# Weights loaded behind the transposes, row and column groups between the layers, and a rebuilt tail: one change to a tuned two-layer attention and expert kernel

## The chip, the cores and the metric

The kernel runs on one core of a Trainium2 chip. The metric is the device time of one execution in microseconds (us); several executions are timed, and the median and the range are given. A trace of one execution (the profile) comes with each kernel. Its span is the time from the first to the last instruction, 1.7 to 1.8 us less than the time of the same execution.

Engines are named as in the profile: PE is TensorE's matmul, PEld its weight load, DVE is VectorE, ACT is ScalarE, POOL is GpSimd, SP is SyncE, which issues most transfers. "L431" is line 431 of the kernel's source. Lines differ between the kernels, so the text names the operation too. In the cuts of code, `ps(...)` reserves a tile of PSUM, into which products are written.

## The reference, cut to what matters

```python
x = A_x                                                         # 2048 rows of 512, bf16
x = x + _A_ref(_layernorm(x, axis=-1), A_wqkv, A_wo)            # linear attention, 32 heads of 16
x = x + _B_ref(_layernorm(x, axis=-1), B_w_r, B_w_gate, B_w_up, B_w_down)
x = x + _A_ref(_layernorm(x, axis=-1), A_wqkv, A_wo)            # the same weights again
x = x + _B_ref(_layernorm(x, axis=-1), B_w_r, B_w_gate, B_w_up, B_w_down)

# in _A_ref: phi(t) = where(t > 0, t + 1, exp(t)) + 1e-6
kv  = einsum("bhsd,bhse->bhde", phi(k), v)                      # K^T V, a sum over all rows
num = einsum("bhqd,bhde->bhqe", phi(q), kv); den = phi(q) . sum(phi(k)); out = (num / den) @ wo
# in _B_ref: the two rows with the largest x @ w_r go through silu(x w_gate) * (x w_up) @ w_down,
# are scaled by a sigmoid and added back to their own rows
```

Each attention layer needs a sum over all rows (K^T V) before any row of its output can be made, and each expert block needs the top two of all 2,048 rows before it can start. So there are four places where everything waits for something small. The last of them, the second expert block, is the tail of the kernel.

## The kernel before

The kernel records every operation with an estimated duration and a weight, and a list scheduler written in Python puts them in one order. That order fixes the order on each engine. The tokens are sixteen tiles of 128 rows. K, Q and O are the products for keys, queries and outputs, four matmuls of 512 columns a tile (0.86 us). K^T V is formed from G, the products of phi(K) with the normalised rows, and from wv after wv has been centred.

The loads. The last number is the earliest planned time, in us; a transpose writes xnT, the operand of K and Q:

```python
for dst, src, key, kb, after in ((wq, A_wq, "wq", 512, 12.0), (wr, B_wrc, "wr", 1, 9.0), (wot, A_wot, "wot", 512, 24.0),
                                 (wv, A_wv, "wv", 512, 26.0), (wo, A_wo, "wo", 512, 28.0)):
    dma(dst[:], src, [key], kb, after)
...
def trans(t, **k):
    def f():
        nc.sync.dma_start_transpose(out=xnT[:, :, t * P : (t + 1) * P], in_=xn[:, t, 0:D])
    op("SP", 1.3, f, r=[("xn", t)], w=[("xnT", t)], lat=1.35, **k)
```

The K^T V product, sixteen products of 128 columns, once a layer:

```python
for c in range(NC):                     # NC = 4
    for k in range(NC):
        T_.matmul(pv[:, c, :].rearrange("p (b f) -> p b f", b=NC), lhsT=wv[:, k, c * P : (c + 1) * P],
            rhs=GT[:, k, :].rearrange("p (b f) -> p b f", b=NC)[:, :, 32 * c : 32 * (c + 1)],
            start=(k == 0), stop=(k == NC - 1))
```

The correction of layer 2's G for the two rows that the first expert block changed: four rows, so products of which TensorE uses 4 of its 128 rows (`4*128` in the timeline below, 0.97 us from the first of them to what follows the last):

```python
pe(4 * MM, lambda: [
    T_.matmul(G2[c]()[:], lhsT=xr4[:, gcol(c) : gcol(c) + P], rhs=pk4[:], start=False, stop=True) for c in range(NC)
], r=["xr4", "pk4"], w=G2)
```

The tail. The output tiles are stored four at a time (512 KB), and the two expert rows, yo, are stored on top of them at the very end, so that store waits for the four large ones:

```python
gu2 = ps("g", [P, 2, NF, 2])
gate_up(gu2, 6, 2)                       # 88 products of 2 columns, gate and up in one PSUM tile
...
for g in (1, 2, 3):
    for i, t in enumerate(ORD[4 * g : 4 * g + 4]):
        last_out(OUTK[g][i], t, prio=1)
    store(ORD[4 * g], ORD[4 * g] + 4)
...
for q in range(NF):                      # down: 44 products in four column groups
    for g in range(NC):
        T_.matmul(yp()[32 * g : 32 * g + 32, :], lhsT=h2[:, q, :], rhs=wd[:, q, g * P : (g + 1) * P],
            start=False, stop=(q == NF - 1), tile_position=(0, 32 * g))
```

## Time and profile before

| | before |
|---|---|
| time, median of 3 runs (range) | 164.12 us (163.51 to 164.63) |
| traced execution | 162.2 us, span 160.5, mean granted TensorE clock 0.969 |
| first K^T V product, layer 1 | 44.79 us |
| first K^T V product, layer 2 | 119.63 us |
| second top-2 (its last step on TensorE starts) | 148.86 us |
| last 512 KB output store issued | 152.20 us |
| expert rows yo being copied out / row store issued | 156.68 / 157.32 us |
| span | 160.49 us |

The page of the kernel before: each digit is the busy share of a fortieth of the span in tenths, PEclk is the granted TensorE clock in tenths, and the last two lines are the chain of work that ended last, by engine and by line.

```profile
PE   6999999589999999999989999999999999996770
DVE  1599999937899999999989988954398999999940
PEclk9999999999999999999999999999999999999755
## 4 chain that ended last, share of the span: by engine, by line
PE 68%; DVE 19%; DMA 5%; ACT 3%; issue 2%; DVEq 0%
```

TensorE is full almost everywhere. It has one hole near slice 7 (28 to 32 us) and a tail from slice 36, where the clock falls as well. The hole is the one wait of TensorE on a transfer. The waits of TensorE from 24 to 46 us:

```profile
PE mm L431 <- DMA xnT<-xn: 2.3, 1, 2.3
```

K of tile 12 (L431) waits 2.3 us for its transpose. The queue of SP shows why: the two 512 KB loads stand between the ninth and the tenth of these transposes. The columns are start, duration, queue and line, operation and count.

```profile
13.03 13.20 SPq L392 DMA_TRANSPOSE xnT<-xn  x9
26.28 0.57 SPq L221 DMA_DIRECT2D wot<-in_A_wot_dram  x1
26.90 0.42 SPq L221 DMA_DIRECT2D wv<-in_A_wv_dram  x1
27.43 8.12 SPq L392 DMA_TRANSPOSE xnT<-xn  x6
35.59 0.57 SPq L221 DMA_DIRECT2D wo<-in_A_wo_dram  x1
```

The timeline of TensorE, five places of it: K of tile 12, the product that centres wv (L757), the first K^T V (L513), the correction of G (L1249) and the second K^T V.

```profile
32.84 1.04 PE L431 MATMUL mm<-wk,xnT 128*128 128x512 bf16 x4 [2.33 <-DMA xnT<-xn]
...
35.44 0.38 PE L757 MATMUL tp<-wv,elast 128*128 128x512 bf16 x1
...
44.79 1.06 PE L513 MATMUL g<-GT,wv 128*128 128x128 bf16 x16
...
116.72 1.03 PE L1249 MATMUL g<-pk,xr 4*128 4x512 bf16 x4
...
119.63 1.05 PE L513 MATMUL g<-GT,wv 128*128 128x128 bf16 x16
```

And the tail: gate and up (L1018), the first part of down (L1416), then down itself after 1.07 us without work, at half clock (granted 0.50 from 150.38 us to the end).

```profile
151.43 2.53 PE L1018 MATMUL g<-xs,wgu 128*128 128x2 bf16 x88
153.90 0.30 PE L1416 MATMUL g<-ident,xf 128*32 128x128 bf16 x4
155.26 1.36 PE L1422 MATMUL g<-wd,h 128*32 128x128 bf16 x44 [1.07 <-DVE h L1411]
```

### The profile page before, as it was taken

What the parts mean: (1) busy time and instruction counts of PE and PEld (TensorE: products, weight loads), DVE (VectorE), ACT (ScalarE), POOL (GpSimd) and SP (SyncE); (2) the same over time, 40 slices, a digit from 0 to 9 for tenths busy, and PEclk for the clock granted to TensorE, in tenths of its full rate; (3) what the DMA queues carried; (4) which work ended last, traced back from release to release, by engine and by line L of the source; (5) the groups of instructions that cost most, each with busy time, mean ns of one, the idle gap of its engine ahead of it and who ended that gap; (6) DMA issues with size and microseconds to landing.
All of it is one profiled execution on the core that took longest, in us unless ns stands there. A gap on an engine that the chain in (4) does not pass through costs nothing.

```text
span 160.5 us, 3799 instructions
## 1 busy us (share of the span) xinstructions
PE 148.6 (93%) x1332; PEld 75.5 (47%) x1332; DVE 132.7 (83%) x481; ACT 108.9 (68%) x263; POOL 23.5 (15%) x66
## 2 busy tenths in 40 slices
PE   6999999589999999999989999999999999996770
PEld 2344444144454444444435445576455455555660
DVE  1599999937899999999989988954398999999940
ACT  3269999625568678889979555543268997798900
POOL 7413113000000000040140300200100000363000
PEclk9999999999999999999999999999999999999755
DMA  4999784978991000033144540000000000012550
GB/s 116 353 355 319 202 97 94 278 152 300 421 432 63 0 0 4 2 64 66 29 73 100 100 99 2 6 0 4 0 0 4 0 4 0 2 50 87 202 192 2
DMA packets 24499, 17.15 MB, mean 107 GB/s; under 512 B 17952, under 2 KB 22560, under 8 KB 24096
## 3 DMA queue, kind: packets, MB, share of 16 engines
q1 hardware_dynamic: 24184, 16.39, 36.1%
q10 hardware_dynamic: 296, 0.53, 1.0%
q8 instruction: 10, 0.16, 0.4%
q14 instruction: 9, 0.07, 0.2%
HBM read 10.62 MB, written 2.10 MB: 79 GB/s over the span
## 4 chain that ended last, share of the span: by engine, by line
PE 68%; DVE 19%; DMA 5%; ACT 3%; issue 2%; DVEq 0%
PE mm L477 15%; PE g L463 13%; PE g L606 9%; PE mm L431 7%; DVE x L615 6%; PE mm L444 5%; DMA xnT<-xn 5%; PE tp L807 3%; DVE pk L409 2%; DVE pq L592 1%; PE g L1018 1%; PE tp L569 1%; PE tp L1018 1%; PE g L551 1%; DVE em L402 1%
## 5 line engine op out<-in xcount | busy, mean ns | idle before, releaser
L398 ACT ACTIVATE e<-mm 128x512 bf16<-128x512 f32 x52 | 30.9, 596 | 18.7 <-PE mm L431 9.9
L463 PE MATMUL g<-pk,xn 128*128 128x512 bf16 x128 | 31.9, 379 | 0.0
L477 PE MATMUL mm<-xnT,wq 128*128 128x512 bf16 x128 | 31.6, 379 | 0.0
L606 PE MATMUL g<-KW,pq 128*128 128x512 bf16 (+1 forms) x132 | 30.2, 372 | 0.0
L431 PE MATMUL mm<-wk,xnT 128*128 128x512 bf16 x80 | 19.9, 379 | 3.0 <-DMA xnT<-xn 2.6
L623 ACT ACTIVATE sq<-x 128x512 bf16<-128x512 bf16 (+1 forms) x33 | 20.1, 612 | 3.1 <-DVE x L615 2.7
L402 DVE TENSOR_SCALAR em<-e 128x512 bf16<-128x512 bf16 x52 | 15.3, 303 | 6.7 <-ACT e L398 6.3
L463 PEld LDWEIGHTS <-xn 128*128 128x128 bf16 x128 | 12.0, 98 | 14.3 <-issue 0.4
L606 PEld LDWEIGHTS <-pq 128*128 128x128 bf16 x132 | 12.4, 97 | 13.2
L477 PEld LDWEIGHTS <-wq 128*128 128x128 bf16 x128 | 11.7, 98 | 12.9 <-issue 0.4
L409 DVE SCALAR_TENSOR_TENSOR pk<-mm,em 128x512 bf16<-128x512 f32 x20 | 13.7, 686 | 0.3
L384 POOL TENSOR_SCALAR xn<-x,s,nb 128x512 bf16<-128x512 bf16 x7 | 5.8, 833 | 56.0 <-DVE nb L371 44.6
L348 DVE BATCH_NORM_STATS2 st<-x 128x6 f32<-128x512 bf16 x16 | 10.3, 677 | 3.3 <-DMA x<-in_A_x_dram 3.3
L431 PEld LDWEIGHTS <-xnT 128*128 128x128 bf16 x80 | 7.3, 97 | 11.9 <-DMA xnT<-xn 4.3
L615 DVE SCALAR_TENSOR_TENSOR x<-x,opr,g 128x512 bf16<-128x512 bf16 (+1 forms) x17 | 11.8, 710 | 0.1
L409 DVE SCALAR_TENSOR_TENSOR pq<-mm,em 128x512 bf16<-128x512 f32 x16 | 10.9, 686 | 0.2
L615 DVE SCALAR_TENSOR_TENSOR x<-x,g 128x512 bf16<-128x512 bf16 x16 | 10.6, 676 | 0.0
L592 DVE TENSOR_TENSOR pq<-pq,rd 128x1024 bf16<-128x1024 bf16 x16 | 10.3, 684 | 0.0
L444 PE MATMUL mm<-wkc,xt 128*128 128x512 bf16 x40 | 9.9, 379 | 0.2 <-DVE pq L409 0.2
L401 ACT ACTIVATE rl<-mm 128x512 bf16<-128x512 f32 x16 | 9.6, 602 | 0.0
L417 ACT ACTIVATE e<-mm,rho 128x512 bf16<-128x512 f32 x12 | 8.3, 689 | 1.6 <-PE mm L450 0.8
L363 ACT ACTIVATE lnv<-mv,eps_t 128x2 f32<-128x2 f32 (+2 forms) x18 | 5.1, 291 | 4.7 <-DVE mv L349 3.9
(249 smaller groups left out, 224.8 us busy)
## 6 DMA issues: line engine op xcount, KB each, us to landing
wgu<-in_B_wgu_dram SPq DMA_DIRECT2D x2, 1408.0 KB, 9.5
out_dram<-pk SPq DMA_DIRECT2D x4, 512.0 KB, 3.2
wd<-in_B_wd_dram SPq DMA_DIRECT2D x1, 1408.0 KB, 13.9
x<-in_A_x_dram SPq DMA_DIRECT2D x4, 256.0 KB, 5.6
xt<-in_A_xt_dram SPq DMA_DIRECT2D x4, 256.0 KB, 5.6
x<-in_A_x_dram SPq DMA_DIRECT2D x2, 512.0 KB, 7.1
wk<-in_A_wk_dram ACTq DMA_DIRECT2D x2, 256.0 KB, 4.1
xt<-in_A_xt_dram SPq DMA_DIRECT2D x1, 512.0 KB, 7.8
```

Of the source, the lines that this page charges most:

```text
L348: dve(0.61, lambda: V.bn_stats(out=st()[:], in_=x[:, t, :]), r=[("x", t)], w=[st]).early = 6.0
L398: act(0.5, lambda: A.activation(out=e()[:], in_=p()[:], func=ACT.Exp), r=[p], w=[e], **k)
L402: dve(0.2, lambda: V.tensor_scalar(out=em()[:], in0=e()[:], scalar1=1.0, scalar2=TINY, op0=ALU.min, op1=ALU.add), r=[e], w=[em], port=True ...
L409: dve(0.6, lambda: V.scalar_tensor_tensor(out=out_ap, in0=p()[:], scalar=0.0, in1=em()[:], op0=ALU.max, op1=ALU.add), r=[p, em], w=[key], **k)
L431: T_.matmul(p()[:], lhsT=xnT[:, c, t * P : (t + 1) * P], rhs=wk[:, c, :], start=(c == 0), stop=(c == NC - 1))
L444: T_.matmul(p()[:], lhsT=xt[:, c, t * P : (t + 1) * P], rhs=w[:, c, :], start=(c == 0), stop=(t >= NM and c == NC - 1),)
L463: T_.matmul(Gs[c]()[:], lhsT=xn[:, t, gcol(c) : gcol(c) + P], rhs=pk[:, t, :], start=first, stop=last)
L477: T_.matmul(p()[:], lhsT=wq[:, i, c, :], rhs=xnT[:, i, j * D : (j + 1) * D], start=(i == 0), stop=(i == NC - 1))
L592: dve(0.6, lambda q=q: V.tensor_tensor(out=q, in0=q, in1=rd()[:].to_broadcast([P, 2, D]), op=ALU.mult), r=[rd], w=[("pq", j, c), ("pq", j, ...
L606: T_.matmul(p()[:, a : a + n], lhsT=pqt(c, t * P, P), rhs=KWs[layer][:, c, a : a + n], start=(c == 0), stop=(c == NC - 1),)
L615: dve(0.04 + 0.6 * n / D, lambda a=a, n=n: V.scalar_tensor_tensor(out=x[:, t, a : a + n], in0=x[:, t, a : a + n], scalar=1.0 if i == 1 els ...
L623: act(0.1 + 0.5 * n / D, lambda a=a, n=n, sq=sq: A.activation(out=sq()[:, 0:n], in_=x[:, t, a : a + n], func=ACT.Square, scale=float(D) ** ...
```

## The change

Its intent: keep large loads out of the way of the transposes; run small products side by side in groups of TensorE's rows or columns; take the patch of x from VectorE; keep TensorE's clock up in the tail; and let SiLU of the gate start while the up products still run. With it came several hundred weights of single operations for the scheduler, found by search, so almost every engine's order differs. Cut to its core:

```diff
-    for ... ((wq, A_wq, "wq", 512, 12.0), ..., (wot, A_wot, "wot", 512, 24.0), (wv, A_wv, "wv", 512, 26.0), (wo, A_wo, "wo", 512, 28.0)):
+    for ... ((wq, A_wq, "wq", 512, 8.0), ..., (wot, A_wot, "wot", 512, 30.0), (wv, A_wv, "wv", 512, 30.0 + 0.5), (wo, A_wo, "wo", 512, 30.0 + 3.0)):
         dma(dst[:], src, [key], kb, after)
     # trans(): the plan now counts a transpose as queued behind loads:  ... lat=1.7).queue = True
@@ K^T V: 32 products of 64 columns, two at a time in two column groups @@
-        p = ps("g")
+        p = ps("g", [P, NC * NC, 1, 16])
         ...
@@ the correction of G: each of its four products in its own group of 32 rows @@
-    pe(4 * MM, lambda: [
-        T_.matmul(G2[c]()[:], lhsT=xr4[:, gcol(c) : gcol(c) + P], rhs=pk4[:], start=False, stop=True) for c in range(NC)
-    ], r=["xr4", "pk4"], w=G2)
+        for c in range(NC):
+            rows = slice(32 * c, 32 * c + 32)
+            T_.matmul(G2[c]()[:], lhsT=xr4[rows, gcol(c) : gcol(c) + P], rhs=pk4[rows, :], start=False, stop=True,
+                tile_position=(32 * c, 0))
@@ the patch of x: VectorE -> ScalarE (out of PSUM) and GpSimd @@
-            V.tensor_tensor(out=xv, in0=xv, in1=pp()[:], op=ALU.add)
+            G_.tensor_tensor(out=xv, in0=xv, in1=ppb[:, j : j + 1, :], op=ALU.add)
@@ the last tile of layer 2 in three pieces, its variance put together in ScalarE's Ln @@
-        parts = ((0, H), (H, H)) if split else ((0, D),)
+        cuts = [0, 256, 384, 512] if split else [0, D]
@@ twelve products on zeros, for the clock alone; gate and up in separate banks, 32 columns wide @@
+    sp_ = ps("mm")
+    for _ in range(12):
+        pe(MM, lambda: T_.matmul(sp_()[:], lhsT=warm[:, 0:P], rhs=warm[:], start=True, stop=True), r=["Odone"], w=[sp_])
-    gu2 = ps("g", [P, 2, NF, 2])
-    gate_up(gu2, 6, 2)
+    gu2 = [ps("g", [P, NF, 32]) for _ in range(2)]
+    gate_up([(p, lambda q, p=p: p()[:, q, :]) for p in gu2], lambda c: xs2[:, c, :], "xs2", 11)
```

## The prediction

> **What bounds the kernel now.** The chain of waits is 68% TensorE, 19% VectorE. Start-to-start gaps of the matmuls show that, from 7 to 145 us, TensorE streams all but about 8.5 us. The windows give three kinds of stage. (a) 24-37 us: TensorE busy 10.5 of 13.0 us. K of tile 12 waits 2.3 us for its DMA transpose, which took 5.4 us to land against a median of 2.5: the 512 KB loads of wot and wv were issued just ahead of it (26.3, 26.9 us). (b) 45-82 and 126-142 us: TensorE and VectorE both full (VectorE 19.9 of 20 us in 62-82). (c) 144.7-160.5 us: a 15.8 us tail of dependent small steps, the granted clock falling to 0.5 at about 150 us.
>
> **What the change does, costed from the trace.**
> 1. wot, wv, wo go behind all sixteen transposes; wq and some x/xt loads change places. In the new SP order the last fourteen transposes are consecutive. At 1.31 us an issue (trace) I estimate tile 12 landing near 31 us instead of 32.8, tile 15 near 35; the first K^T V product then starts near 43 us instead of 44.8. **-1.8 us**, all critical.
> 2. K^T V product in two column groups: 16 x 56 ns = 0.89 us becomes an estimated 0.6, twice. **-0.6 us**.
> 3. The four-row correction of G becomes four row groups: now 4 x 216 ns plus a switch, 0.97 us; concurrent, about 0.35. **-0.6 us**. [...] the trace agrees for column groups: starts 3-4 ns apart, about 60 ns for four.
> 4. x patch from VectorE to ScalarE and GpSimd: 1.4 us of VectorE where it is idle: **0**.
> 5. New order by many weights: stages 45-119 hold about 3.5 us of TensorE gaps; I give it **-0.6 us**.
> 6. Tail. Twelve idle matmuls and 32-column gate/up products should keep the clock at 1.0: down product 1.36 to about 0.9 us, gate/up 2.45 to 2.2. Separate banks let SiLU overlap the up products: 1.3 us between gate/up and down becomes about 0.5. Three pieces and the shorter variance path gain little: VectorE is last there, and added small steps and an output tile stand in its queue. But the final row-store waits for the last 512 KB output store, landed at 157.2 us, as late as the row itself: this caps the gain. **-1.3 us**.
>
> Sum: -4.9 us, so 159.2 us.
>
> **Chances.** 80% range 156.0-162.0. Faster by over 2% (below 160.8): 0.74; within 2%: 0.24; slower: 0.02.
>
> **What would show each step.** (1) K waiting on transposes under 1.2 us, K^T V starting at 42-43.5 us, transposes landing in about 2.5 us. (2) 32 products of 64x64 in about 0.6 us. (3) Row-group products starting a few ns apart, 0.35 us in all. (4) GpSimd's patch done before the first layer-2 denominators. (5) VectorE still 98% busy after the first layer's products. (6) Clock 1.0 to the end; under 0.7 us from last up product to first down product; final row-store issued when the last output store lands.
>
> **What would make it wrong.** wv landing too late, so that the centring product, ahead of two G products in TensorE's queue, stalls it. xt or x of late tiles, issued 4-6 us later, stalling K. The GpSimd patch delaying layer 2. The clock falling all the same. A better order in 45-142 us than I credit: two to three us faster. VectorE's queue delaying the last variance: up to 0.6 us slower.

The 0.35 us of step 3 is an estimate from the trace of before: a 512-column product takes 216 ns, four products of 512 columns in column groups start 3 to 4 ns apart with the next one 217 or 206 ns after the fourth (L551, 122.8 to 123.3 us), and the two intervals around the four-row products are about 90 ns longer than usual (311 ns before the first, 306 after the last). That row groups behave like column groups was not shown there, nor that idle matmuls or 32-column products hold the clock.

## The result

| | before | after | after, second run (c_after) |
|---|---|---|---|
| median (range) | 164.07 us (163.51 to 164.63, 4 runs) | 158.67 us (157.58 to 159.27, 4 runs) | 158.21 us (157.80 to 158.66, 4 runs) |
| traced span, clock | 160.49, 0.969 | 156.90, 0.992 | 155.97, 0.995 |
| first K^T V, layer 1 | 44.79 | 43.16 | 42.42 |
| first K^T V, layer 2 | 119.63 | 116.32 | 115.50 |
| second top-2 | 148.86 | 146.17 | 145.33 |
| last 512 KB store issued | 152.20 | 148.92 | 148.08 |
| yo / row store issued | 156.68 / 157.32 | 153.23 / 153.71 | 151.73 / 152.79 |

The ratio of after to before is 0.966, 95% interval 0.960 to 0.973. A ratio is the mean time of one kernel's fast runs over that of the other's in the same rounds, so it is not quite the ratio of the medians quoted. On the chip of the second run, before took 163.17 us (161.19 to 165.52) and the ratio was 0.975 (0.965 to 0.986). Medians and ranges here and below are of all executions; the ratios leave out those that the record calls slow (three of the seven of before on that chip).

The page of the changed kernel, the lines that were shown of before:

```profile
PE   6989999997999999999999999999999999998970
DVE  1799999776699999999999979853488999999840
PEclk9999999999999999999999999999999999999996
## 4 chain that ended last, share of the span: by engine, by line
PE 72%; DVE 12%; DMA 5%; ACT 5%; issue 3%; SPq 0%; ACTq 0%; DVEq 0%
```

The hole at slice 7 is gone and a shallower one stands at slice 9; the clock holds to the last slice (granted 1.00 until 154.24 us, where it was 150.38). TensorE's waits from 24 to 46 us, and SP's queue:

```profile
PE tp L792 <- DMA wv<-in_A_wv_dram: 1.1, 1, 1.1
```

```profile
13.76 20.48 SPq L402 DMA_TRANSPOSE xnT<-xn  x14
34.29 0.57 SPq L230 DMA_DIRECT2D wv<-in_A_wv_dram  x1
34.92 0.41 SPq L230 DMA_DIRECT2D wot<-in_A_wot_dram  x1
35.38 0.43 SPq L230 DMA_DIRECT2D wo<-in_A_wo_dram  x1
```

The fourteen transposes now go through without a load among them. K of tile 12 starts 3.0 us earlier and waits for nothing, but wv is issued at 34.29 us, and the centring product, moved back in TensorE's order, waits for it. The five places of TensorE's timeline again:

```profile
29.84 1.03 PE L441 MATMUL mm<-wk,xnT 128*128 128x512 bf16 x4
...
38.90 0.38 PE L792 MATMUL tp<-wv,elast 128*128 128x512 bf16 x1 [1.13 <-DMA wv<-in_A_wv_dram]
...
43.16 0.75 PE L525 MATMUL g<-GT,wv 128*64 128x64 bf16 x32
...
113.96 0.40 PE L1294 MATMUL g<-pk,xr 32*128 32x512 bf16 x4
...
116.33 0.69 PE L525 MATMUL g<-GT,wv 128*64 128x64 bf16 x32
```

The correction of G takes 0.40 us instead of 1.03, and K^T V 0.75 and 0.69 instead of 1.06 and 1.05. The tail:

```profile
148.62 2.35 PE L1059 MATMUL g<-xs,wgu 128*128 128x32 bf16 x88 [0.25 <-DVE xs L1417]
150.91 0.24 PE L1476 MATMUL g<-ident,xf 128*32 128x128 bf16 x4
151.64 0.69 PE L1482 MATMUL g<-wd,h 128*32 128x128 bf16 x36 [0.49 <-DVE h L1470]
152.89 0.29 PE L1482 MATMUL g<-wd,h 128*32 128x128 bf16 x8 [0.57 <-issue]
```

Between gate/up and down 0.49 us are idle where it was 1.07, and down runs at full clock (1.00; its groups of four start 56 ns apart, in before 107), but it stops after its 36th product for a reason that the profile can only call "issue". SiLU starts at 150.35 us, 0.45 us before the last up product starts; in before it starts 0.63 us after that (154.43, 153.80). Now, where did the 4 us come from? Subtracting the milestones of the tables:

| stretch | before | after | c_after |
|---|---|---|---|
| start to first K^T V, layer 1 | 44.79 | 43.16 (-1.63) | 42.42 (-2.37) |
| to first K^T V, layer 2 | 74.84 | 73.16 (-1.68) | 73.08 (-1.76) |
| to second top-2 | 29.23 | 29.85 (+0.62) | 29.83 (+0.60) |
| to yo | 7.82 | 7.06 (-0.76) | 6.40 (-1.42) |
| to row store | 0.64 | 0.48 (-0.16) | 1.06 (+0.42) |
| to the end | 3.17 | 3.19 | 3.18 |
| sum | 160.49 | 156.90 (-3.6) | 155.97 (-4.5) |

Two things stand out. Layer 2 up to the second top-2 became slower. And in the second trace, where down did not stop, yo was ready 0.7 us sooner against the top-2, but the row store gained nearly nothing from it: it was waiting for something else.

The two medians differ by more (5.4 us) than the spans. The fast executions of before that were not traced had lower mean clocks than the traced one: 0.955 to 0.965 in the last set of eleven, against 0.969. One more stretch of 3.41 us at half clock, as e_loads_first has one below, lowers the mean over 162 us by 0.5 x 3.41 / 162 = 0.01, so I estimate that before loses up to one such stretch more in many of its runs. No trace of before itself shows one; e_loads_first and b_loads_late show one and two behind a stop of TensorE.

### The profile page after: what moved, and what is told of

Same layout as the page of the kernel before. It is cut to its first block, busy times and chain, and to the rows that moved or that the text cites. A ratio compares the mean times of both kernels' runs of the same rounds, so it can differ in the third digit from the quotient of the medians.

```text
span 156.9 us, 3902 instructions
## 1 busy us (share of the span) xinstructions
PE 147.9 (94%) x1380; PEld 74.4 (47%) x1380; DVE 130.2 (83%) x481; ACT 111.9 (71%) x272; POOL 28.5 (18%) x78
## 4 chain that ended last, share of the span: by engine, by line
PE 72%; DVE 12%; DMA 5%; ACT 5%; issue 3%; SPq 0%; ACTq 0%; DVEq 0%
PE mm L487 18%; PE g L473 17%; PE g L618 11%; PE mm L441 10%; DVE x L628 4%; PE mm L454 4%; DMA wv<-in_A_wv_dram 3%; ACT pk L1334 3%; DMA x<-in_A_x_dram 3%; DVE st L358 2%; DVE pq L604 2%; PE tp L581 1%; PE tp L1059 1%; PE g L563 1%; PE mm L597 1%
## 5 line engine op out<-in xcount | busy, mean ns | idle before, releaser
L408 ACT ACTIVATE e<-mm 128x512 bf16<-128x512 f32 x52 | 30.4, 597 | 12.7 <-PE mm L441 6.7
L618 PE MATMUL g<-KW,pq 128*128 128x512 bf16 (+2 forms) x136 | 30.6, 366 | 0.4 <-DVE x L628 0.4
L636 ACT ACTIVATE sq<-x 128x512 bf16<-128x512 bf16 (+2 forms) x34 | 20.4, 601 | 2.9 <-DVE x L628 2.5
L394 POOL TENSOR_SCALAR xn<-x,s,nb 128x512 bf16<-128x512 bf16 x6 | 4.9, 825 | 52.9 <-PE g L618 37.9
L628 DVE SCALAR_TENSOR_TENSOR x<-x,opr,g 128x512 bf16<-128x512 bf16 (+2 forms) x18 | 11.9, 684 | 0.4 <-PE g L618 0.3
L373 ACT ACTIVATE lnv<-mv,eps_t 128x2 f32<-128x2 f32 (+3 forms) x18 | 5.2, 291 | 5.0 <-DVE mv L359 3.3
```

The source lines that it names most:

```text
L408: act(0.5, lambda: A.activation(out=e()[:], in_=p()[:], func=ACT.Exp), r=[p], w=[e], **k)
L618: T_.matmul(p()[:, a : a + n], lhsT=pqt(c, t * P, P), rhs=KWs[layer][:, c, a : a + n], start=(c == 0), stop=(c == NC - 1),)
L628: dve(0.04 + 0.6 * n / D, lambda q=q, a=a, n=n: V.scalar_tensor_tensor(out=x[:, t, a : a + n], in0=x[:, t, a : a + n], scalar=1.0 if i == ...
L636: act(0.1 + 0.5 * n / D, lambda q=q, a=a, n=n, sq=sq: A.activation(out=sq()[:, 0:n], in_=x[:, t, a : a + n], func=ACT.Square, scale=float( ...
```

## The experiments

All kernels were correct. Each was timed against before on its own chip, so ratios compare best; differences from the changed kernel are read from the traces.

### e_loads_first: the load order undone

wot and wv go back in front of the eleventh transpose. All else stays as in the changed kernel, the late centring product too.

```diff
+        trs = [o for o in seq if o.eng == "SP" and o.w and o.w[0][0] == "xnT"]
+        for key in ("wot", "wv"):
+            o = next(o for o in seq if o.w == (key,))
+            seq.remove(o)
+            seq.insert(seq.index(trs[10]), o)
```

> The changed kernel with one thing undone: the loads of wot and wv stand again ahead of the last six transposes in the SP queue (wo stays behind). Every other engine's order is the same. Theory (step 1 is worth 1.8 us because late loads free the transposes): K of a late tile waits 1.5 to 3 us for its transpose again, the centring product no longer waits for wv, so the first K^T V product starts at 44.0 to 45.0 us instead of 43.2, and the time rises by 1.0 to 1.8 us. Rival (the new order of the other engines, not the load order, made the gain): the first K^T V product starts at 42.5 us or before and the time falls, because wv is no longer waited for.

Measured: 162.61 us (161.33 to 164.40), ratio to before 1.004 (0.992 to 1.016). The gain of the whole change is gone. K of tile 12 waits 2.9 us (2.3 in before), and then something more happens: the first K^T V starts at 46.81 us, 3.65 us later than in the changed kernel and 2 us later than in before. The waits of TensorE from 24 to 50 us, and the windows:

```profile
PE mm L442 <- DMA xnT<-xn: 2.9, 1, 2.9
```

```profile
core 0: us, PE busy (x) PEld busy (x) DVE busy (x) ACT busy (x) POOL busy (x), PEclk, DMA share, GB/s
...
34.00:38.00 4.00, 4.00 (x12) 1.47 (x11) 0.98 (x2) 1.15 (x2) 0.00 (x0) 0.57 0.70 183
```

After the stop of TensorE (3.0 us from one product's start to the next beyond the usual gap) the granted clock is 0.5 from 34.1 to 37.5 us, 3.41 us in which a 512-column product takes 426 ns instead of 215. So this stop cost itself and then half of that stretch, 1.7 us, again. The 2.3 us stop of before cost nothing of the kind: the clock record of its trace stands at 1.00 from 7.02 to 150.38 us. These are single cases; no run shows how long a stop may be. The load order was worth about 4 us here, more than twice what I had predicted.

### e_wv_early: wv from another queue

In the changed kernel wv is loaded from ScalarE's queue at about 20 us, so that it goes ahead of the late transposes without standing in SP's order. In the trace of after the DMA engines are busy for 0.45 of the time from 18 to 24 us.

```diff
+        o = next(o for o in seq if o.w == ("wv",))
+        seq.remove(o)
+        o.fn = lambda: nc.scalar.dma_start(out=wv[:], in_=A_wv)
+        seq.insert(next(i for i, q in enumerate(seq) if q.eng == "ACT" and q.start > 20.0), o)
```

> The changed kernel with the load of wv alone issued at about 20 us from ScalarE's queue, in the stretch where the transposes leave the DMA engines half idle. Theory (the load of wv, queued behind the last transposes, is what the centring product and so all of TensorE waits for, 1.6 us): that wait goes, the first K^T V product starts at 41.5 to 42.2 us instead of 43.2, and the time falls by 1.0 to 1.6 us. Rival (the transposes cannot bear 512 KB among them): a K waits for its transpose by 1 us or more and the K^T V start stays at 43 us.

Measured: 157.98 us (157.89 to 158.09), ratio 0.978 (0.972 to 0.983). TensorE waits for no transfer between 24 and 46 us, and the first K^T V starts at 42.23 us: 0.9 us before the trace of the changed kernel, but only 0.2 us before its second trace, in which the wait for wv was 0.2 us instead of 1.1. So the wait is real but varies, and taking it out is worth 0.2 to 0.9 us, less than the 1.0 to 1.6 expected. K of tile 12 starts at 30.16 us, as in c_after (30.02), so the early load got in no transpose's way.

### e_rows_off: the correction of G in one row group

```diff
-                G2[c]()[:], lhsT=xr4[rows, gcol(c) : gcol(c) + P], rhs=pk4[rows, :], start=False, stop=True,
-                tile_position=(32 * c, 0),
+                G2[c]()[:], lhsT=xr4[0:4, gcol(c) : gcol(c) + P], rhs=pk4[0:4, :], start=False, stop=True,
```

> The changed kernel with the four-row correction of G as four products one after the other on rows 0 to 3, no row groups; all orders the same. Theory: the four products take 0.97 us again instead of 0.33, and everything after them starts 0.6 us later, so +0.6 us in the span of the stretch from the correction to the second K^T V product. Rival (they were not on the critical chain, or the switch cost eats the gain): under 0.3 us.

Measured: 159.54 us (158.15 to 159.97), ratio 0.986 (0.976 to 0.996). From the correction to the second K^T V it is 3.00 us instead of 2.36: the row groups are worth 0.64 us, as predicted. In all ten traces that have both kinds of groups this stretch is 2.36 or 2.37 us. The switch that the prediction and the expectation name stands on both sides with and without row groups: the last start before the four comes 310 ns ahead of them in after and 311 in before, where 215 is usual, and the next start 319 ns after the last of the four in after, 306 in before, instead of 216. In after the four start 3 to 4 ns apart. The whole times of this run and the next are not clear enough of noise to show as little.

### e_cols_off: K^T V without column groups

The sixteen products of 128 columns and their mask are put back.

```diff
-        p = ps("g", [P, NC * NC, 1, 16])
+        p = ps("g")     # and the sixteen products of before
```

> The changed kernel with K^T V as before: sixteen 128-column products instead of thirty-two 64-column ones in two column groups, twice; all orders the same. Theory: each K^T V takes 0.84 us from first to last start instead of 0.55 and 0.50, +0.3 us each; but the grouped form pays a switch of about 0.1 us on each side, so the net is +0.1 to +0.25 us each, +0.2 to +0.5 us in all. Rival (prediction's 0.3 each without switches): +0.6 us in all.

Measured: 159.72 us (158.89 to 160.08), ratio 0.988 (0.980 to 0.995). From the first K^T V product to the first O product it is 7.85 us instead of 7.50 in layer 1 and 7.93 instead of 7.68 in layer 2, 0.6 us in all, as predicted. The switch on each side, in the trace of after: the first product of K^T V starts 308 and 309 ns after the 512-column product before it instead of 215, and the product behind it 130 and 129 ns after its last start, where its pairs start about 32 ns apart. This trace has a stop of 0.9 us at 80 us besides, in front of a K product, which I don't put down to the edit.

### c_after: the changed kernel again

No edit; it stands beside the next three on one chip.

> Control: the changed kernel itself, unaltered, on the chip and in the rounds of the tail experiments. Expected: 157.5 to 159.3 us; in its trace again a stop of 0.4 to 0.8 us after the 36th of the 44 down products, at the same place of TensorE's program (theory: TensorE's instructions run out there[...]). Rival: the stop was a chance event of one execution and is not seen again.

Measured: 158.21 us (157.80 to 158.66), ratio 0.975 (0.965 to 0.986). The stop after the 36th down product, 0.79 us in the first trace, isn't there, against the expectation: down takes 0.66 us from its first to its last start, and yo starts to be copied out at 151.73. But the row store goes out at 152.79, so the end of the kernel moved only by what had been gained before the tail (0.84 us at the last output store).

### e_no_spin and e_no_spin_narrow: the tail without the twelve products on zeros

```diff
-        pe(MM, lambda: T_.matmul(sp_()[:], lhsT=warm[:, 0:P], rhs=warm[:], start=True, stop=True), r=["Odone"], w=[sp_])
+        pe(MM, lambda: None, r=["Odone"], w=[sp_])
@@ e_no_spin_narrow, besides @@
-    gate_up([(p, lambda q, p=p: p()[:, q, :]) for p in gu2], lambda c: xs2[:, c, :], "xs2", 11)
+    gate_up([(p, lambda q, p=p: p()[:, q, 0:2]) for p in gu2], lambda c: xs2[:, c, 0:2], "xs2", 11)
```

> The changed kernel without the twelve idle matmuls of the tail; all other orders the same. Theory: with nothing dense after the last O product the clock falls to 0.5 at 148 to 149.5 us instead of 150 to 153.6; gate/up takes 2.4 us or more instead of 2.2 and the groups of four down products 100 ns instead of 60: 0.4 to 0.8 us longer from the second top-k to the last down product, apart from the stop inside the down products, which should go because TensorE's program is 24 rows shorter (that gives back 0.4 to 0.8, so the total time may hardly move). Rival: the 32-column gate/up products alone hold the clock, and gate/up stays at 2.2 us.

> The changed kernel without the twelve idle matmuls and with gate/up products of 2 columns as before. Theory: the clock is as in the kernel before, mean 0.96 to 0.975, gate/up 2.4 us or more, down groups about 105 ns; 0.5 to 0.9 us slower than without the idle matmuls removed, less the stop. If this equals the run without idle matmuls alone, the 32 columns do nothing for the clock by themselves; if that one keeps the clock and this one does not, they do.

Measured: 158.71 us (158.64 to 158.91) and 158.29 us (157.97 to 159.34), ratios 0.978 and 0.974. Without the twelve products the clock falls to half at 144.3 us (145.3 in the narrow one; I had expected 148 to 149.5) and stays there to the end. The clock line of e_no_spin's page:

```profile
PEclk9999999999999999999999999999999999998555
```

The second top-2 to yo takes 7.50 us instead of 6.40. So they hold the clock here (1.00 in c_after from 140 to 153 us), and that is worth 1.1 us of the chain. The whole time shows no more than half of it: the second top-2 came 0.2 us sooner (29.65 instead of 29.83 us after the second K^T V), and yo has some 0.7 us of slack before the row store in c_after. In both runs the row store goes out 0.13 us after the last 512 KB store has landed, so what the clock is worth once the store is on time was not measured. The 32 columns instead of 2 did nothing measurable here; with the twelve products they were not tried alone.

### e_up_first: the up products ahead of the gate products

All up products of layer 2 are issued ahead of all gate products, so that the separate banks let nothing start early.

```diff
+            if layer2[0]:
+                part = todo[NF:] + todo[:NF] if lo == 0 else []
```

> The changed kernel with the 44 up products ahead of the 44 gate products, so that SiLU can start only after all 88, as when both lay in one bank; all other orders the same. Theory: the time from the last of the 88 products to the first down product grows from 0.83 us to 1.6 to 1.9 us, and the row is stored 0.8 to 1.1 us later; the total time rises by 0.5 to 1.1 us (part may hide behind the last output store). Rival (the ScalarE queue, whose table load and tanh end at 150.4 us, sets when SiLU starts, so the bank split gains little): under 0.4 us.

Measured: 158.10 us (157.75 to 158.30), ratio 0.974 (0.963 to 0.984), the same as c_after. And yet the edit did what it should: from the last gate/up product to the first down product it is 1.78 us instead of 0.84. A delay of 0.94 us in the last chain of the kernel cost nothing that the time shows. So in c_after the chain of small steps did not set the end. What did is the wait for the last 512 KB store: the row store follows its issue by 4.72 us in c_after, and by 4.85 here, where yo starts to be copied out 0.33 us before the row store. In both it goes out 0.13 us after that store has landed; here yo is finished only 0.05 us before it, so the delay has just used up the slack. The queue of SP, from 145 us on, waits for the store before the row store can go (first c_after, then e_up_first):

```profile
SPq L1498 <- DMA out_dram<-pk: 2.8, 1, 2.8
```

```profile
SPq L1500 <- DMA out_dram<-pk: 2.9, 1, 2.9
```

### What holds the last store

That led me to look at the transfers, which I had treated as a fixed latency. The moved data of the changed kernel, in forty slices from the issue of the last output store to that of the row store:

```profile
GB/s 324 341 375 290 384 265 256 290 410 384 299 401 410 384 282 358 341 299 367 282 375 282 256 26 9 26 26 26 17 26 26 26 26 26 17 9 0 0 0 0
...
q8 instruction: 1, 0.02, 1.1%
```

A slice is 0.12 us. For 2.8 us the transfers run at some 340 GB/s, 0.95 MB in all: what is left of the output stores before, and the last one behind it. Then 1.4 us follow at about 22 GB/s, a sixteenth of it, which I read as one of the 16 DMA engines still at work while the others have finished. Each store ends with sixteen 4-byte packets. In the ten traces (before, after twice, and the seven experiments above) fifteen of them are done 2.6 to 2.9 us after the issue and the sixteenth at 4.2 to 4.6 us. The row store goes out about 0.55 us after the sixteenth. And in each of the ten traces one packet of 16 KB on an "instruction" queue lies within that store, and takes 0.88 to 1.57 us:

| | 16 KB packet took | 15 engines done | 16th engine done |
|---|---|---|---|
| before | 1.57 | 2.62 | 4.57 |
| after | 0.88 | 2.83 | 4.25 |
| c_after | 0.88 | 2.85 | 4.20 |
| e_no_spin | 1.24 | 2.84 | 4.47 |

(us after the issue of the last output store, except for the packet's duration.) The engine is late by the packet's time and some 0.4 to 0.5 us more. There are ten such packets in a trace (queue 8: `q8 instruction: 10, 0.16` on the page; the other instruction queue, 14, carried packets of up to 8 KB), and TensorE has by far the most instructions, 2,760 on the page of the changed kernel (1,380 products, each with its weight load; the next is VectorE with 481), so I took them for TensorE's. That could be tested.

### x_warm_30: forty TensorE instructions more at the very start

The ten warm-up products of 512 columns become thirty of 170, the same number of columns less 20. The programs of all other engines and the rest of TensorE's are the same, instruction for instruction.

```diff
-            for _ in range(n):
-                T_.matmul(p()[:], lhsT=warm[:, 0:P], rhs=warm[:], start=True, stop=True)
+            for _ in range(3 * n):
+                T_.matmul(p()[:, 0:170], lhsT=warm[:, 0:P], rhs=warm[:, 0:170], start=True, stop=True)
```

> The changed kernel with the ten warm-up products of 512 columns at the very start cut into thirty of 170 columns: the same work, and 40 more TensorE instructions ahead of all others, so that everything counted in TensorE instructions comes 40 instructions earlier in the program. In ten traces, of before and after alike, fifteen of the sixteen transfer engines finish the last 512 KB output store 2.6 to 2.9 us after its issue and the sixteenth at 4.2 to 4.6, and each time a 16 KB instruction packet took 0.88 to 1.57 us within the store. Theory (the packet brings TensorE's next instructions and holds up one engine): the packet comes at least 0.5 us earlier against the last store's issue than in the changed kernel (where it came 1.0 to 1.7 us after it); if it comes before the three last stores it leaves no late engine, all sixteen finish by 3.0 us after the issue, and the row store follows the issue by 3.4 to 4.2 us instead of 4.7 to 4.8, or waits only for the down product; the stop of TensorE after the 36th down product is gone or has moved by about 20 products. Rival (one engine is always late with the last store, the packet is by chance): the sixteenth engine finishes at 4.2 us or later wherever the packet is. If the packet stays in the same place against the stores, nothing is told apart.

Measured: 156.39 us (156.34 to 156.77), ratio 0.962 (0.956 to 0.967), the fastest kernel: 3.8% less than before, and 1.6 us less than e_two_pieces on the same chip. The last packet now comes 2.8 us ahead of the last output store's issue, and an eleventh after the end of the stores. Only TensorE's program had changed, so these packets are TensorE's. It moved by more than the 20 products that were added: from its predecessor it is 133 products (266 instructions) away here, but 196 in c_after (counted by weight loads, of which no record is missing). So in c_after the packet came some 60 products later in TensorE's program, an estimate from 196 less 133; what it waited for there no view shows. All sixteen engines are done 2.88 us after the issue. The moved data of this kernel, from the issue of the last output store to that of the row store (a slice is 0.10 us):

```profile
GB/s 359 338 348 338 348 338 348 264 243 338 380 380 338 370 338 338 348 359 348 338 338 348 359 359 348 359 359 254 127 11 0 0 0 0 0 0 0 0 169 0
```

The 22 GB/s are gone. The row store goes out 3.88 us after the last output store instead of 4.72, and 0.32 us after yo instead of 1.06: it now waits for its data last, as the queue of SP from 145 us on shows.

```profile
SPq L1498 <- DMA out_dram<-pk: 1.4, 1, 1.4
SPq L1498 <- DVE yo L1494: 0.5, 1, 0.5
```

Down runs without a stop, and the mean clock of the span is 1.000. TensorE's tail in this kernel:

```profile
147.37 2.35 PE L1059 MATMUL g<-xs,wgu 128*128 128x32 bf16 x88 [0.24 <-DVE xs L1417]
149.65 0.24 PE L1476 MATMUL g<-ident,xf 128*32 128x128 bf16 x4
150.38 0.80 PE L1482 MATMUL g<-wd,h 128*32 128x128 bf16 x44 [0.49 <-DVE h L1470]
```

Of the 1.24 us that this trace is shorter than that of c_after, 0.84 are this, and 0.4 were there before the last output store (the first K^T V at 42.05 us instead of 42.42), which I don't put down to the edit.

### x_warm_30_up_first: the gate and up order once more

> The kernel with thirty short warm-up products (156.39 us, the row store 0.32 us behind its data, all sixteen transfer engines done 2.9 us after the last store's issue) with one more edit: all up products of layer 2 before all gate products, so that the separate banks let nothing start early. With the store late, the same edit cost nothing (158.10 us against 158.21), though it put the down products 0.94 us later. Theory (the new order of gate and up is worth 0.9 us, and the late store had hidden it): the instruction packet stays before the three stores, gate/up to down 1.7 to 1.8 us instead of 0.84, the row store 0.8 to 1.0 us later against the last output store's issue (4.7 to 4.9 us), and the whole 157.1 to 157.5 us. Rival (the order of gate and up is worth nothing even then, something else holds the row store): the whole within 0.3 us of 156.4.

The edits are those of x_warm_30 and e_up_first together. Measured: 157.51 us (157.26 to 157.71, 6 runs), ratio 0.972 (0.966 to 0.978). Gate/up to down is 1.79 us instead of 0.84, all sixteen engines are done 2.89 us after the issue, and the row store follows the last output store by 4.84 us, 0.32 us after yo. The same edit that cost nothing in c_after costs 1.1 us here. So gate ahead of up, each in its own tile of PSUM, is worth about 1 us, and in the changed kernel as it stands the late engine hides it.

### b_loads_late: the load order alone, in the kernel before

wot and wv go behind the transpose of tile 14; nothing else of before changes, so its centring product still stands early in TensorE's order.

```diff
+        moved = [next(o for o in seq if o.w == (key,)) for key in ("wot", "wv")]
+        reader = next(o for o in seq if "wv" in o.r and o.eng == "PE")
+        for o in moved:
+            seq.remove(o)
+        k = seq.index(reader)
+        seq[k:k] = moved
```

> The kernel before, with one part of the change alone: the loads of wot and wv go behind the transpose of tile 14 (one transpose, that of tile 15, still follows), everything else as it was, so the centring product that reads wv still stands early in TensorE's order. Theory (the load order is worth something only together with the later place of wv's first reader): K of tile 12 no longer waits 2.3 us for its transpose, but the centring product stops TensorE until wv lands at about 38 us instead of 35.4, so the first K^T V starts at 47 to 48 us (44.8 in the kernel before) and the whole is 2 to 5 us slower than the kernel before. Rival (moving the loads is a gain by itself, 1.8 us as predicted): first K^T V at about 43 us and a ratio near 0.99.

A first build (not kept in the record), with the loads behind the transpose of tile 15 too, was REFUSED by the check, since the centring product would have been issued before the load of what it reads. Measured: 167.24 us (166.11 to 168.53), ratio 1.028 (1.020 to 1.036). K of tile 12 starts at 29.48 us, 3.4 us sooner than in before, and all of that is lost again at the centring product. The waits of TensorE from 24 to 50 us:

```profile
PE tp L758 <- DMA wv<-in_A_wv_dram: 5.8, 1, 5.8
```

The clock is then 0.5 from 34.9 to 41.7 us, twice 3.41 us, and the first K^T V starts at 48.94 us, a microsecond later than I had expected. So the load order by itself is a loss of 2.8%. It is a gain only together with the later place of wv's first reader, which came with the new weights.

### e_two_pieces: the last tile in two pieces instead of three

```diff
-        cuts = [0, 256, 384, 512] if split else [0, D]
+        cuts = [0, 256, 512] if split else [0, D]
```

> The changed kernel with the last tile of layer 2 in two pieces (256 + 256 columns) instead of three (256 + 128 + 128), all else the same as far as the plan allows. Theory (pieces that share one accumulation bank wait for one another, so the third piece brings nothing): from the last K^T V of layer 2 to the last piece's product 25.4 us or less instead of 25.8, and the last output store is issued at the same time or up to 0.4 us earlier; the whole is within 0.4 us of the changed kernel. Rival (three pieces shorten the statistics of the last tile, as predicted): the last piece's residual and square take twice as long, 0.2 to 0.4 us later at the second top-k, the whole 0.3 us slower.

Measured: 157.96 us (157.89 to 158.53), ratio 0.972 (0.966 to 0.977). The last product of the tile starts 24.79 us after the second K^T V instead of 25.78, and the residual is done at 141.79 us instead of 142.40. Even so, ScalarE starts the last statistic at 144.00 us in both (143.97 in c_after): VectorE's queue, with a 0.42 us maximum and output tiles in front of the small steps, is what it waits for, so the number of pieces makes no difference to it. The theory holds for that; in c_after the product of the third piece waits 0.40 us for VectorE's residual of an earlier piece, a wait that is not there with two. It missed at the top-2, which came 0.57 us later than in c_after, because the plan put an output tile and three small steps in front of one copy on VectorE; the rival had it 0.2 to 0.4 us later for another reason. The edit also moved the twelve products on zeros: they come earlier, and none is left behind the second top-2, where TensorE then has nothing to do for 0.73 us. The clock is 0.5 from 147.6 to 151.0 us, and falls again at 154.4 us; the page of this run shows both in its last slices:

```profile
PEclk9999999999999999999999999999999999999967
```

So the twelve products held the clock where they stood between the small steps, and moved away from there they did not. The whole time is the same as c_after's, but here too the row store goes out 0.13 us after the last 512 KB store has landed, so the time can't tell what two pieces would be worth.

## Why the prediction was right, and where it was not

The time was predicted at 159.2 us and came to 158.67, and the chance of a gain over 2%, 0.74, fell on the right side. That the time came so close is partly luck: the sum hides three terms that were off.

1. **"wot, wv, wo go behind all sixteen transposes ... -1.8 us, all critical."** The first K^T V moved by -1.63 and -2.37 us in the two traces, so the size looks right, but it is a difference of larger things. K of tile 12 moved by 3.0 us. The wait for wv, which the prediction named only as a risk ("wv landing too late, so that the centring product ... stalls it"), took up to 1.1 us back. And the term is not separable: undone alone it costs about 4 us (e_loads_first), done alone it loses 2.8% (b_loads_late), because the stops of 3.0 and 5.8 us in these two runs also cost 3.41 and 6.83 us at half clock. That second cost was missing from my sum, and it is probably why the medians differ by a microsecond or more beyond the spans; for before that is an estimate.
2. **K^T V in column groups, -0.6 us.** Shown: 0.35 + 0.25 us (e_cols_off). From its first to its last start a K^T V takes 0.55 and 0.50 us instead of 0.84 and 0.83.
3. **The correction of G in row groups, -0.6 us.** Shown: 0.64 us (e_rows_off).
4. **The patch of x, 0.** The two GpSimd tiles were done before layer 2's denominators, and no engine waited for them. The trace of after shows it; no run isolates it.
5. **"New order by many weights ... -0.6 us."** Between the two K^T V the change gained 1.68 us; less 0.64 for the rows and 0.35 for the columns, 0.7 us is left for the order. But from the second K^T V to the second top-2 it lost 0.62 us although the columns gain 0.25 there, so 0.85 us went to the order and to the new operations. The twelve products account for 0.2 us of this (e_no_spin). The pieces matter too: the last O product starts 24.8 us after the second K^T V in before, 25.8 in after and c_after, and 24.8 again in e_two_pieces, though the columns of the O and Q products in this stretch are the same. So three pieces instead of two put it 1.0 us later; how much of that reaches the top-2 is not shown, since e_two_pieces lost more behind it. The rest isn't settled: the prediction's "VectorE's queue delaying the last variance: up to 0.6 us slower" fits it, and so does VectorE's order in e_two_pieces. In sum this term is near zero or slightly a loss, not -0.6.
6. **The tail, -1.3 us, capped by the last output store.** From the second top-2 to yo it gained 1.42 us in c_after. Undone one at a time, the clock is worth 1.1 us of that stretch (e_no_spin) and the order of gate and up 0.9 (e_up_first); neither edit gives quite the arrangement of before (its clock fell later, and its products lay better than with up first), so the two do not add up to the gain. The cap was right, and it took 0.42 us back. What I had wrong is what the cap is made of. The prediction treats the landing of the store, about 5 us after its issue, as given. It is 3.2 us when no instruction packet is in the way (x_warm_30; the packets are done after 2.9); the 1.3 to 2.0 us that the sixteenth engine takes longer in the other traces are one DMA engine late by a 16 KB block of TensorE's instructions. With that gone, the tail shortens the run as the change meant it to.

So the mechanism of steps 2, 3, 4 and of the clock in step 6 was right with its size; step 1 was the right place with an incomplete account; step 5 was mis-sized; and the sum came out because the missing costs of step 1 lie on before's side while the loss before the second top-2 lies on after's.

The stop after the 36th down product was there in three traces of the changed kernel's program length (0.79 us in after, 0.81 in e_wv_early, 0.41 in e_rows_off), always at the same product, with the 16 KB packet starting 1.5 us or more after the last store's issue; TensorE went on about 1.5 us after the packet had ended. In c_after and e_loads_first the packet started some 0.5 us earlier, and the same step took 0.12 and 0.11 us instead of 0.05. I read this as TensorE running out of instructions, since gate/up uses them up at 25 ns a product (88 starts in 2.18 us in after) and the profile names no other wait. One run, though not made for it, moves the place: e_two_pieces has four O products fewer (132 instead of 136), and its stop, 0.34 us, stands after the 40th down product, four later. With 12 or 32 products fewer (the two kernels without the twelve products, and e_cols_off) the place would lie behind the last down product, and nothing stops; in x_warm_30 the packet came long before. In e_up_first, which has the same number of products, the packet was late too, but down started 1 us later and came to the place 1.6 us after the packet's end. So the place goes with the count of TensorE's instructions; no run was made to move it on purpose, and the reading stays an estimate.

## What to carry to other kernels

Before a load is moved out of the way of something urgent, look up its own first reader and move that too: here the load order alone lost 2.8%. Look at the clock behind every long stop of TensorE: here a stop of 3.0 us cost 3.41 us at half clock besides, one of 5.8 us twice that, and one of 2.3 us none. The length of the stop does not settle it: in the tails of before and of e_two_pieces the clock fell behind stops of no more than 0.75 us between small products. When a chain of small steps at the end of a kernel has been made faster and the time does not follow, find what the last instruction really waits for by delaying the chain on purpose: if a delay costs nothing, it's the other branch. Look at transfers per engine and not only per transfer: here a rate that fell from some 340 to 22 GB/s and stayed there for 1.4 us was one late engine of sixteen, and the reason was a 16 KB packet of the program's own instructions, whose place 40 more instructions at the very start moved.
